# Earlier and later places for small VectorE work: the statistics of row tiles 4 and 5 and the parameters' reciprocals in a fused S4 and feed-forward kernel

## The chip, the cores and the metric

The kernel runs on one core of one Trainium2 chip. The metric is the device time of one execution in microseconds (us). A separate profiled execution gives the trace: every instruction with its engine (PE is TensorE, DVE is VectorE, ACT is ScalarE, POOL is GpSimd, SP issues DMAs), its line in the kernel, its start and its length.

## The reference

With x of 2048 rows and 576 columns, the kernel returns the sum of three terms: x, a state-space convolution of its normalised rows, and a feed-forward layer of the same rows.

```python
xn = layernorm(x)                                  # rows of 576, no scale, no shift
# S4: 128 complex states for each of the 576 channels
dt = exp(log_dt);  K[d, l] = Re(sum_n C[d, n] * dt*B[d, n] * exp(dt*A[d, n] * l))
y  = irfft(rfft(xn, 2L) * rfft(K, 2L))[:L] + xn * Dskip
# feed-forward with 4608 hidden units
f  = silu(xn @ w1) @ w2
return x + y + f
```

All inputs and outputs are float32.

## The kernel before

**The feed-forward part** sets the pace. The 2048 rows are 16 tiles of 128 rows (j = 0 to 15), in two halves of eight; a block is four tiles (512 rows). For each half, nine chunks of the hidden units are walked, each with FT = 4 groups of 128. Step `up` (lines 321 to 337) multiplies one group of w1 with a block into the PSUM tile `ph`; step `down` (338 to 356) multiplies the results with w2 into `po`, twice 288 columns for each row tile, twelve matmuls each, and VectorE adds `po` into the tile `acc` (L356).

Every product is done in three parts, since the matmul type keeps fewer bits than float32: an operand is split into a high part, rounded by ScalarE, and a low part, which VectorE obtains as a difference. So a group of w2 is loaded into `w2r` (L302, on SP's queue, two buffers), ScalarE writes `w2h` (L311), VectorE writes `w2l` (L313), and the result of `up` goes through silu `gf` (L334), `gh` (L335) and `gl` (L337). A `w2r` buffer is free for the next load when its `w2h` and `w2l` are done. The first chunk's four groups of w2 are the ones that the change calls the second weights.

**Rows.** Each pair of tiles is loaded from `x` into `acc`. `norm` (L185 to 206) takes the statistics (bn_stats L192, four for a pair; bn_aggr L193), adds epsilon (L196), has GpSimd raise to the power of -1/2 (L197) and normalises (`xn`, VectorE L201 or ScalarE L206). TensorE transposes `xn` (L124, L131), and the copies are split again (`xh` L125, `xl` L126, `x4` L133 and L134). `phase0` does that for the tiles of the first half: 0 and 1, 2 and 3, 4 and 5, 6 and 7. `late(j)` does the same for the tiles 8 to 15 (tiles `xj`, `tr`), which are written to memory for later.

**Side work.** `side` produces all other work as a generator, which `weave` runs along the feed-forward steps: each `yield` gives the share of the 288 steps at which the next part is to be emitted. `natural` computes, on tiles of 96 partitions with 6 x 128 elements (parameter layout), the magnitude, phase and decay of the S4 parameters: products and absolute values, the smaller over the larger one (three reciprocals of 96x256 each, L522; multiplied L523; cut at one L524; its square plus one L526, L527), then decays from tanh (ScalarE L531 reciprocal square root, L532 square, VectorE L535 to L537, stored by SP), then the arctangent (ScalarE L544) and the reciprocal square root (L546) of the ratio. Each `yield` in it ends a stage; the list at the end of the block below (line 906) says at which step each stage (`nt`) and each part of the late tiles (`tiles`) is emitted. `gate_of(0)`, `gate_of(1)` and `gate_of(2)` are the steps 5, 13 and 21 of 288. After it come the generator of the kernel K (`kgen`, from share 0.13) with the transform of the rows (`spread`), the product of spectra (`spectral`) and the inverse transform.

**What sets the order.** A scheduler with a timeline of its own arranges each engine's instructions when the program is built; the order on an engine is then fixed. `behind(pin)` demands that the instructions in it be issued after the instruction that is kept in `pins` under a name: `pins["xt3"]` is the last `xl`-like difference of tile 3 (L134), `pins["w2l"]` the last low part of w2 emitted so far, `pins["gl"]` and `pins["gh"]` the last results of `up`. Work inside `tc.high_priority()` (L334 to L337, L356) goes ahead of other work that is ready. ScalarE needs another table for silu than for the arctangent, and the program has an instruction (ACT_TABLE_LOAD) wherever the table changes.

Of the kernel before, what the change touches and what calls it, by code (L numbers as in the profile page):

```python
# [15 lines left out]
ALU = mybir.AluOpType  # L16
# [10 lines left out]
HD = D // 2  # L27
# [16 lines left out]
def kernel(  # L44
# [21 lines left out]
    nc = tc.nc  # L66
    FT = 4
    NCH = NFT // FT
# [43 lines left out]
    acc = {}  # L112
# [26 lines left out]
    pins = {}  # L139

    def behind(ins):
        return tc.issue_after(ins) if ins is not None else nullcontext()
# [24 lines left out]
    def load_x(j, pool, tag, engines):  # L167

        t = pool.tile([P, 2, D], F32, tag=tag, name=f"{tag}{j}")
        for i in range(2 if j == 0 else 1):  # L170
            for ps, v, eng in quarters(xv, engines):
                if j:
                    eng.dma_start(t[ps], v[:, j:j + 2])
                else:
                    eng.dma_start(t[ps, i], v[:, i])
        pairs[j] = t
        return t[:, 0, :], t[:, 1, :]
# [78 lines left out]
    def ffn():  # L256
# [82 lines left out]
        def down(blk, jj):  # L339
            half, c, b = blk  # L340
            j = 8 * half + 4 * b + jj
            js = slice(jj * P, (jj + 1) * P)
            if half == 1 and c == NCH - 1:
                if jj % 2 == 0:
                    add_conv(j, (acc[j], acc[j + 1]))
            for h in range(2):
                hs = slice(h * HD, (h + 1) * HD)
                po = ps2.tile([P, 512], F32, tag="ps2", name="po")
                n = 0
                for t in range(FT):  # L350
                    for g, w in ((0, 0), (0, 1), (1, 0)):
                        pins["pe"] = nc.tensor.matmul(po[:, :HD], G[blk, t][g][:, js], W2[half, c, t][w][:, hs],  # L352
                                                      start=n == 0, stop=n == 3 * FT - 1).ins
                        n += 1
                with tc.high_priority():
                    nc.vector.tensor_add(acc[j][:, hs], po[:, :HD], acc[j][:, hs])  # L356
            if half == 0 and c == NCH - 1:
                rows = slice(j * P, (j + 1) * P)
                nc.sync.dma_start(dr0[rows, :], acc[j])
                if j % 2:  # L360
                    acc[7 + j], acc[8 + j] = load_x(7 + j, accp, "acc", (nc.sync,))
# [103 lines left out]
    def natural(nat, par):  # L465

        fT, phiT = kf["f"], kf["phi"]
        NT, NP = 6, 96
        v = nc.vector
# [19 lines left out]
        br, bi = load(b_re, "br"), load(b_im, "bi")  # L489
# [18 lines left out]
        pr, pi, t0, t1 = tl("pr"), tl("pi"), tl("t0"), tl("t1")  # L508
# [9 lines left out]
        v.tensor_tensor(br, cr, ci, op=ALU.max)  # L518
        v.tensor_tensor(bi, cr, ci, op=ALU.min)
        v.tensor_scalar(t0, br, 1e-37, None, op0=ALU.max)  # L520
        for i in range(0, NT, 2):
            v.reciprocal(t0[:, i:i + 2], t0[:, i:i + 2])  # L522
        v.tensor_mul(t0, t0, bi)  # L523
        v.tensor_scalar(t0, t0, 1.0, None, op0=ALU.min)  # L524

        v.tensor_mul(t1, t0, t0)  # L526
        v.tensor_scalar(t1, t1, 1.0, None, op0=ALU.add)  # L527
        yield

        with behind(pins["gh"]):  # L530
# [2 lines left out]
        for i in range(0, 4 * D, D):  # L533
# [4 lines left out]
            v.scalar_tensor_tensor(r[:, c], e, 2.0, r[:, c], op0=ALU.add, op1=ALU.mult)  # L538
            v.scalar_tensor_tensor(ex[:, c], ex[:, c], 1.0, r[:, c], op0=ALU.add, op1=ALU.mult)
        nc.sync.dma_start(dexp, ex[:, :3 * D].rearrange("n (d k) -> n d k", k=3))  # L540
        yield

        with behind(pins["gh"]):
# [289 lines left out]
    def add_conv(j, dsts):  # L833

        py = [pool.tile([P, 512], F32, tag=t, name="py") for pool, t in ((pss, "pss"),) * 3 + ((ps2, "ps2"),)]
        first = pins["pe"]
        for n in range(16):
            i, q1, q2, h = 1 - n // 8, n // 4 % 2, n // 2 % 2, 1 - n % 2
            o = 64 * q1 + 32 * q2
            rows = slice(64 * h, 64 * h + 64)  # L840
            with tc.high_priority() if n else nullcontext(), behind(first):
                mm = nc.tensor.matmul(py[2 * i + h][o:o + 32, :HD], s4[rows], yss[j + i][rows, 2 * q2 + q1],  # L842
                                      start=True, stop=True, tile_position=(64 * h, o), skip_group_check=True)
            if n == 0:
                first = mm.ins
        for i in range(2):
            del yss[j + i]
            for h in range(2):
                hs = slice(h * HD, (h + 1) * HD)
                nc.vector.tensor_add(dsts[i][:, hs], py[2 * i + h][:, :HD], dsts[i][:, hs])  # L850
        for _ in range(2):
            conv_load()

    def gate_of(i):

        return (FT + i * 2 * FT + 1) / (2 * NCH * 2 * 2 * FT)

    def side():
        nonlocal s4, kl, yp, pa, tail_at
        marks = (0.13, 0.597, 0.823)  # L860
        tail_at = (0.91, 0.934, 0.967, 0.0072)
        with tc.tile_pool(name="kf", bufs=1) as kfp:
            for n in ("f", "phi"):
                kf[n] = kfp.tile([P, D], F32, name=n + "T")
            with tc.tile_pool(name="par", bufs=1) as par:
                with tc.tile_pool(name="pa", bufs=4) as pa:

                    zero = pa.tile([P, 512], BF16, name="zero", bufs=1)
                    nc.vector.memset(zero, 0.0)
                    pz = ps1.tile([P, 512], F32, tag="ps1", name="pz")  # L870

                    def idle(n):
                        for _ in range(n):
                            nc.tensor.matmul(pz, zero[:, :P], zero, start=True, stop=True)

                    idle(12)
                    p01, p23 = phase0(pa, (0, 1), idle), phase0(pa, (2, 3))
                    next(p01)
                    yield 0
                    next(p23)  # L880
                    yield 0
                    next(p01)
                    yield 0
                    next(p23)
                    yield 0
                    for js in ((4, 5), (6, 7)):
                        with behind(pins["xt3" if js[0] == 4 else "w2l"]):
                            for _ in phase0(pa, js):
                                pass
                    kf["dt"] = steps()  # L890
                    for n, ap in (("are", a_re), ("aim", a_im)):
                        kf[n] = par.tile([96, 6, NS], F32, tag=n, name=n)
                        nc.sync.dma_start(kf[n], ap.rearrange("(p t) n -> p t n", t=6))
                    yield 0
                with tc.tile_pool(name="nat", bufs=1) as nat, tc.tile_pool(name="pb", bufs=1) as pb:
                    nt = natural(nat, par)
                    def late(j):

                        xs = load_x(j, pb, "xj", (nc.sync,))
                        yield  # L900
                        with behind(pins["xn" if j == 8 else "gl"]):
                            normed(pb, (j, j + 1), xs)
                        yield

                    tiles = chain.from_iterable(late(j) for j in range(8, NJ, 2))
                    for at, todo in ((0.0, nt), (0.0, tiles), (0.004, tiles), (0.005, tiles), (gate_of(0), nt), (0.026, tiles), (0.028, tiles), (0.036, tiles), (0.038, tiles), (gate_of(1), nt), (0.06, tiles), (gate_of(2), nt), (0.09, nt)):
                        yield at
                        with behind(pins["gl"] if at else pins["xt7"] if todo is nt else None):
                            next(todo, None)
            with behind(pins["sd"]):  # L910
                nc.gpsimd.dma_start(f1, cf1)
            nc.sync.dma_start(vt, cv)
            with tc.tile_pool(name="up", bufs=1) as up:
                sp = spread(up)
                for n, at in enumerate(kgen()):
                    if n > 1:
                        next(sp, None)
                    yield marks[0] + at * (marks[1] - marks[0])
                for _ in sp:
                    pass  # L920
        s4p = ctx.enter_context(tc.tile_pool(name="s4p", bufs=1))
        s4 = s4p.tile([P, 32], F32, name="s4")
        nc.gpsimd.dma_start(s4, cs4)

        with tc.tile_pool(name="kl", bufs=2) as kl:
            for at in spectral():
                yield marks[1] + (at - 1) * (marks[2] - marks[1])
        yp = ctx.enter_context(tc.tile_pool(name="yp", bufs=3))
        yield from tail()

    sd = side()
    fg = ffn()
    for g in (sd, fg, sd, fg, sd, fg, sd, fg, sd):
# [84 lines left out]
```

## Time and profile before

| | us |
|---|---|
| median of three runs | 1111.88 (1111.85 to 1111.98) |
| the profiled execution | 1111.65 |
| its span, first to last instruction | 1109.9 |
| TensorE busy in the span | 1101.6 (99%) |
| VectorE busy | 916.1 (83%) |
| ScalarE busy | 707.3 (64%) |
| GpSimd busy | 71.0 (6%) |

The span is 1.75 us shorter than the profiled execution's own time, which is 0.23 us below the median of the runs. Times in the trace count from the start of the span. A row of a timeline gives start, length (of several merged instructions, from the first start to the last end), engine, line, operation, output and inputs, partitions x elements, count, and, in brackets, the idle time of the engine ahead of it with what ended it. Matmuls overlap: the time that one takes from the path is the distance from its start to that of the next.

### The profile page before, as it was taken

The page shows a single profiled execution, that of the slowest core. Times are in us where ns is not written, and L with a number is a line of the kernel's source. Part 1 is how long each engine was busy: PE and PEld are TensorE (multiplying, and loading weights), DVE is VectorE, ACT ScalarE, POOL GpSimd, SP SyncE. Part 2 cuts the span into 40 slices and gives each one's busy share as a digit, 9 for nine tenths or more (in the row PEclk, how much of TensorE's full clock was granted, in tenths as well). Part 3 has the DMA queues.
Part 4 walks back from the last instruction along what each step waited for, and adds up shares of the span by engine and source line. Part 5 has one row for each costly group of instructions (what it writes and reads, how often), then busy time and mean ns, then how long its engine had stood idle before and what let it go on. Part 6 is the DMA issues. An engine that isn't in the chain of part 4 may idle for free.

```text
span 1109.9 us, 22912 instructions
## 1 busy us (share of the span) xinstructions
PE 1101.6 (99%) x9167; PEld 997.5 (90%) x9167; DVE 916.1 (83%) x1542; ACT 707.3 (64%) x1223; POOL 71.0 (6%) x127
## 2 busy tenths in 40 slices
PE   8999999999999999999999999999999999999998
PEld 6988999899889899899989989999999999999887
DVE  7799899999999999999999837787778778784433
ACT  4574466676677676677866536877777778774210
POOL 1100000000000000011000000000000000000111
PEclk9999999999999999999999999999999999999999
DMA  8745522425242525255734163554544445434973
GB/s 255 205 123 154 146 61 61 120 72 126 77 109 82 130 62 130 77 154 163 209 127 105 44 177 105 168 159 126 160 145 150 139 147 170 130 107 130 257 205 87
DMA packets 175851, 148.56 MB, mean 134 GB/s; under 512 B 111088, under 2 KB 142720, under 8 KB 175616
## 3 DMA queue, kind: packets, MB, share of 16 engines
q1 hardware_dynamic: 165408, 112.69, 37.8%
q0 software_dynamic: 9504, 33.49, 9.5%
q8 instruction: 72, 1.18, 0.5%
q10 hardware_dynamic: 832, 0.92, 0.3%
q14 instruction: 35, 0.29, 0.1%
HBM read 102.53 MB, written 44.61 MB: 133 GB/s over the span
## 4 chain that ended last, share of the span: by engine, by line
PE 97%; DMA 2%; SPq 0%; DVE 0%; ACT 0%; issue 0%; ACTq 0%
PE po L352 42%; PE ph L326 35%; PE kp L691 3%; PE ph L327 3%; PE ph L328 3%; PE pu L821 2%; PE pb L821 2%; PE pk L821 2%; PE z L706 2%; PE pu L160 1%; PE py L842 1%; PE pu L161 1%; DMA acc<-in_A_u_dram 1%; DMA w2r<-in_B_w_dram 1%; DMA w1r<-in_B_w_dram 0%; PE ptk L485 0%
## 5 line engine op out<-in xcount | busy, mean ns | idle before, releaser
L352 PE MATMUL po<-w2l,gh 128*128 128x288 f32 x1152 | 338.6, 296 | 1.2 <-DVE w2l L313 1.2
L352 PE MATMUL po<-w2h,gl 128*128 128x288 f32 x1152 | 336.6, 295 | 0.0
L352 PE MATMUL po<-w2h,gh 128*128 128x288 f32 x1152 | 336.4, 296 | 0.0
L352 PEld LDWEIGHTS po<-w2h,gh 128*128 128x128 f32 x1152 | 215.3, 188 | 7.6 <-issue 2.8
L352 PEld LDWEIGHTS po<-w2l,gh 128*128 128x128 f32 x1152 | 216.0, 188 | 6.5 <-DVE w2l L313 1.4
L352 PEld LDWEIGHTS po<-w2h,gl 128*128 128x128 f32 x1152 | 215.6, 188 | 0.9
L334 ACT ACTIVATE gf<-ph 128x512 f32<-128x512 f32 (+1 forms) x148 | 86.3, 584 | 145.3 <-PE ph L328 133.0
L326 PE MATMUL ph<-xh,w1h 128*128 128x512 f32 (+1 forms) x592 | 161.6, 387 | 0.3 <-ACT xh L125 0.3
L326 PE MATMUL ph<-xl,w1h 128*128 128x512 f32 (+1 forms) x592 | 161.5, 386 | 0.0
L326 PE MATMUL ph<-xh,w1l 128*128 128x512 f32 (+1 forms) x592 | 161.2, 385 | 0.0
L356 DVE TENSOR_TENSOR acc<-po,acc 128x288 f32<-128x288 f32 x288 | 126.9, 454 | 36.9 <-PE po L352 35.6
L337 DVE TENSOR_TENSOR gl<-gf,gh 128x512 fp32r<-128x512 f32 (+1 forms) x148 | 99.4, 675 | 64.5 <-ACT gh L335 63.7
L326 PEld LDWEIGHTS ph<-xh,w1l 128*128 128x128 f32 x592 | 108.1, 188 | 19.9
L326 PEld LDWEIGHTS ph<-xl,w1h 128*128 128x128 f32 x592 | 108.0, 188 | 20.0 <-DVE xl L126 0.2
L326 PEld LDWEIGHTS ph<-xh,w1h 128*128 128x128 f32 x592 | 104.6, 188 | 17.1 <-ACT xh L125 0.8
L335 ACT CAST gh<-gf 128x512 fp32r<-128x512 f32 (+1 forms) x148 | 89.6, 609 | 9.5 <-PE po L352 6.6
L648 ACT ACTIVATE c<-th,magic 128x1040 f32<-128x1040 f32 x36 | 42.1, 1169 | 37.7 <-DVE C L671 27.7
L650 ACT ACTIVATE c<-th 128x1040 f32<-128x1040 f32 x36 | 38.7, 1075 | 34.1 <-DVE th L649 34.1
L311 ACT CAST w2h<-w2r 128x576 fp32r<-128x576 f32 x72 | 47.0, 671 | 16.7 <-PE po L352 14.9
L292 DVE TENSOR_TENSOR w1l<-w1r,w1h 128x640 fp32r<-128x640 f32 x72 | 57.2, 823 | 0.2
L327 PE MATMUL ph<-x,w1h 128*128 128x512 f32 (+1 forms) x148 | 57.1, 386 | 0.0
L328 PE MATMUL ph<-x,w1l 128*128 128x512 f32 (+1 forms) x148 | 56.9, 385 | 0.0
(182 smaller groups left out, 1829.3 us busy)
## 6 DMA issues: line engine op xcount, KB each, us to landing
w2r<-in_B_w_dram SPq DMA_DIRECT2D x72, 288.0 KB, 3.7
w1r<-in_B_w_dram SPq DMA_DIRECT2D x35, 512.0 KB, 3.7
d1u<-u POOLq DMA_DIRECT2D x32, 288.0 KB, 2.5
d1k<-stage SPq DMA_DIRECT2D x18, 512.0 KB, 7.0
ur<-d1u SPq DMA_DIRECT2D x32, 288.0 KB, 3.4
kr<-d1k SPq DMA_DIRECT2D x32, 288.0 KB, 2.8
d<-yo POOLq DMA_DIRECT2D x32, 288.0 KB, 3.6
ys<-d SPq DMA_DIRECT2D x32, 288.0 KB, 10.7
```

Source lines behind the costliest of these rows:

```text
L292: pins["w1l"] = nc.vector.tensor_sub(l1, src, h1).ins
L311: pins["w2h"] = nc.scalar.copy(h2, r2).ins
L326: nc.tensor.matmul(ph, w[:, kt, :], v[:, kt, a:e], start=n + kt == 0, stop=False)
L327: nc.tensor.matmul(ph, h1[:, 4, :], x4[:, a:e], start=False, stop=False)
L328: pins["pe"] = nc.tensor.matmul(ph, l1[:, 4, :], x4[:, a:e], start=False, stop=True).ins
L334: nc.scalar.activation(gf, ph, AF.Silu)
L335: pins["gh"] = nc.scalar.copy(gh, gf).ins
L337: pins["gl"] = nc.vector.tensor_sub(gl, gf, gh).ins
L352: pins["pe"] = nc.tensor.matmul(po[:, :HD], G[blk, t][g][:, js], W2[half, c, t][w][:, hs], start=n == 0, stop=n == 3 * FT - 1).ins
L356: nc.vector.tensor_add(acc[j][:, hs], po[:, :HD], acc[j][:, hs])
L648: nc.scalar.activation(c65, th, AF.Identity, bias=magic)
L821: nc.tensor.matmul(dst, st, mv[:, hs], start=n == 0, stop=n == 3 * len(terms) - 1)
```

## The change

Two pieces of VectorE work get other places. The statistics, normalisation and transposes of tiles 4 and 5 were to be issued behind the last difference of tile 3; now they are issued behind the low parts of the first four groups of w2, as those of tiles 6 and 7 already were. In `natural`, the three reciprocals and the four operations behind them leave the end of the second stage and become a stage of their own behind the decays and their store. That stage has a new entry in the list, three steps after `gate_of(1)` (step 16 of 288), and is issued behind the newest sum of an output into `acc` (L356), which is now kept in `pins["acc"]`. The arithmetic is the same.

```diff
@@ down
                 with tc.high_priority():
-                    nc.vector.tensor_add(acc[j][:, hs], po[:, :HD], acc[j][:, hs])
+                    pins["acc"] = nc.vector.tensor_add(acc[j][:, hs], po[:, :HD], acc[j][:, hs]).ins
@@ natural
         v.tensor_scalar(t0, br, 1e-37, None, op0=ALU.max)
-        for i in range(0, NT, 2):
-            v.reciprocal(t0[:, i:i + 2], t0[:, i:i + 2])
-        v.tensor_mul(t0, t0, bi)
-        v.tensor_scalar(t0, t0, 1.0, None, op0=ALU.min)
-
-        v.tensor_mul(t1, t0, t0)
-        v.tensor_scalar(t1, t1, 1.0, None, op0=ALU.add)
         yield
...
         nc.sync.dma_start(dexp, ex[:, :3 * D].rearrange("n (d k) -> n d k", k=3))
+        yield
+        for i in range(0, NT, 2):
+            v.reciprocal(t0[:, i:i + 2], t0[:, i:i + 2])
+        v.tensor_mul(t0, t0, bi)
+        v.tensor_scalar(t0, t0, 1.0, None, op0=ALU.min)
+
+        v.tensor_mul(t1, t0, t0)
+        v.tensor_scalar(t1, t1, 1.0, None, op0=ALU.add)
         yield
@@ side
                     for js in ((4, 5), (6, 7)):
-                        with behind(pins["xt3" if js[0] == 4 else "w2l"]):
+                        with behind(pins["w2l"]):
@@ side, the list: one entry more behind (gate_of(1), nt)
+                    (gate_of(1) + 3 / (4 * NCH * 2 * FT), nt)
-                        with behind(pins["gl"] if at else pins["xt7"] if todo is nt else None):
+                        with behind(pins["acc" if todo is nt and at == gate_of(1) + 3 / (4 * NCH * 2 * FT) else "gl"] if at else pins["xt7"] if todo is nt else None):
                             next(todo, None)
```

More of the change, by code (lines that the diff above doesn't have):

```diff
@@ L905, in side @@
                     tiles = chain.from_iterable(late(j) for j in range(8, NJ, 2))
-                    for at, todo in ((0.0, nt), (0.0, tiles), (0.004, tiles), (0.005, tiles), (gate_of(0), nt), (0.026, tiles), (0.028, tiles), (0.036, tiles), (0.038, tiles), (gate_of(1), nt), (0.06, tiles), (gate_of(2), nt), (0.09, nt)):
+                    for at, todo in ((0.0, nt), (0.0, tiles), (0.004, tiles), (0.005, tiles), (gate_of(0), nt), (0.026, tiles), (0.028, tiles), (0.036, tiles), (0.038, tiles), (gate_of(1), nt), (gate_of(1) + 3 / (4 * NCH * 2 * FT), nt), (0.06, tiles), (gate_of(2), nt), (0.09, nt)):
                         yield at
-                        with behind(pins["gl"] if at else pins["xt7"] if todo is nt else None):
+                        with behind(pins["acc" if todo is nt and at == gate_of(1) + 3 / (4 * NCH * 2 * FT) else "gl"] if at else pins["xt7"] if todo is nt else None):
                             next(todo, None)
```

## The prediction

> **What bounds the kernel now.** I read the page first: busy times, the granted clock, the chain that ended last, the DMA issues.
>
> ```profile
> PE 1101.6 (99%) x9167; PEld 997.5 (90%) x9167; DVE 916.1 (83%) x1542; ACT 707.3 (64%) x1223; POOL 71.0 (6%) x127
> ...
> PEclk9999999999999999999999999999999999999999
> ...
> PE 97%; DMA 2%; SPq 0%; DVE 0%; ACT 0%; issue 0%; ACTq 0%
> ...
> w2r<-in_B_w_dram SPq DMA_DIRECT2D x72, 288.0 KB, 3.7
> ```
>
> TensorE bounds it: 99% of the span busy, 97% of the last chain. A change of VectorE's order is worth only what TensorE waits for today, less what it makes TensorE wait for tomorrow. So next TensorE's waits over the whole run (waiter, releaser; us in total, times, longest), and TensorE's busy time in five stretches.
>
> ```profile
> PE pz L874 <- DVE zero L869: 1.3, 1, 1.3
> PE pt L124 <- DVE xn L201: 1.2, 1, 1.2
> PE po L352 <- DVE w2l L313: 1.2, 1, 1.2
> PE ph L326 <- ACT xh L125: 0.3, 1, 0.3
> ```
>
> ```profile
> 0.00:25.00 25.00, 20.88 (x132) 1.00 0.86 251
> 25.00:140.00 115.00, 115.00 (x707) 1.00 0.60 161
> 140.00:660.00 520.00, 520.00 (x5348) 1.00 0.40 107
> 660.00:1000.00 340.00, 340.00 (x2150) 1.00 0.48 145
> 1000.00:1110.00 110.00, 105.75 (x838) 1.00 0.67 171
> ```
>
> All four waits lie in the first 25 us; from 25 to 1000 us TensorE has no gap. The change touches one of the four, the third. Last the timeline around it, TensorE, then VectorE, then ScalarE's casts.
>
> ```profile
> 23.16 0.28 PE L328 MATMUL ph<-x,w1l 128*128 128x256 f32 x1
> 23.28 0.30 PE L352 MATMUL po<-w2h,gh 128*128 128x288 f32 x1
> 24.76 0.40 PE L352 MATMUL po<-w2l,gh 128*128 128x288 f32 x1 [1.18 <-DVE w2l L313]
> 25.00 0.29 PE L352 MATMUL po<-w2h,gl 128*128 128x288 f32 x1
> 25.13 0.30 PE L352 MATMUL po<-w2h,gh 128*128 128x288 f32 x1
> ```
>
> ```profile
> 20.35 0.42 DVE L134 TENSOR_TENSOR x<-pt,x 64x256 fp32r<-64x256 f32 x1
> 22.51 1.54 DVE L192 BATCH_NORM_STATS2 st<-acc 128x6 f32<-128x288 f32 x4 [1.74 <-DMA acc<-in_A_u_dram]
> 23.96 2.08 DVE L313 TENSOR_TENSOR w2l<-w2r,w2h 128x576 fp32r<-128x576 f32 x3
> 26.08 0.71 DVE L313 TENSOR_TENSOR w2l<-w2r,w2h 128x576 fp32r<-128x576 f32 x1
> 26.70 1.18 DVE L192 BATCH_NORM_STATS2 st<-acc 128x6 f32<-128x288 f32 x3
> 28.22 0.75 DVE L337 TENSOR_TENSOR gl<-gf,gh 128x256 fp32r<-128x256 f32 x2
> ```
>
> ```profile
> 19.55 2.40 ACT L311 CAST w2h<-w2r 128x576 fp32r<-128x576 f32 x4
> ```
>
> VectorE was free at 20.77 (20.35 + 0.42), idled 1.74 us for the rows of tile 4, did their statistics, and only then wrote the first w2 low part. TensorE wanted that at 23.41 (23.28 plus the pitch of 0.13 between 25.00 and 25.13) and started at 24.76.
>
> **The change part by part.** *Statistics of tiles 4 and 5.* Nothing is removed; 4 bn_stats, 2 bn_aggr and what follows go behind the four `w2l`. The casts they need end one after the other between 19.55 and 21.95, so some 0.6 us each: the first is there at about 20.2, and VectorE can start at 20.8. One `w2l` is worth 0.7 us (2.08 / 3), so the first is done at about 21.5, 1.9 us ahead of 23.41, and the last at 23.6. The wait goes. Its worth is the lost pitch: 24.76 - 23.28 - 0.13 = 1.35 us. (The matmul after the stop also began 0.24 instead of 0.13 later; that could add 0.11, which I leave in the range.)
>
> What is late next: tile 4's statistics run from 23.6 to 25.2, tile 6's and 7's after them until about 26.8, and then the `gl` that stood at 28.22. If the rows of tiles 6 and 7 came only when VectorE used them (26.70, without a wait), the `gl` would stay where it was, at 28.2 to 29.0. TensorE now does 22 output matmuls, not 9, between the first weights' products and the next group, and by their 0.13 us reaches these `gl` at about 29.1. Covered at either end, by 0.1 us in the bad one; cover gone, it costs at most 1.2 us, the size of the waits seen. The loads on SP's queue stand in the same sequence; GpSimd's two powers keep theirs. Cost: nothing.
>
> *The reciprocals.* Rows of VectorE, ScalarE, SP's queue and TensorE where the old place was and the new one is:
>
> ```profile
> 67.67 4.96 DVE L522 RECIPROCAL t<-t 96x256 f32<-96x256 f32 x3
> ...
> 78.07 0.94 DVE L523 TENSOR_TENSOR t<-t,bi 96x768 f32<-96x768 f32 x1
> ...
> 84.26 0.74 DVE L313 TENSOR_TENSOR w2l<-w2r,w2h 128x576 fp32r<-128x576 f32 x1
> ```
>
> ```profile
> 86.69 1.28 ACT L544 ACT_TABLE_LOAD   x1
> 87.99 0.85 ACT L544 ACTIVATE t<-t 96x768 f32<-96x768 f32 x1
> 88.74 0.66 ACT L311 CAST w2h<-w2r 128x576 fp32r<-128x576 f32 x1
> ...
> 93.08 1.28 ACT L334 ACT_TABLE_LOAD   x1
> 94.37 0.60 ACT L334 ACTIVATE gf<-ph 128x512 f32<-128x512 f32 x1
> ```
>
> ```profile
> 85.03 2.27 SPq L302 DMA_DIRECT2D w2r<-in_B_w_dram  x2
> ```
>
> ```profile
> 91.39 0.29 PE L352 MATMUL po<-w2h,gh 128*128 128x288 f32 x1
> ...
> 96.37 1.09 PE L326 MATMUL ph<-xh,w1h 128*128 128x512 f32 x4
> ```
>
> The work is equal: 4.96 us of reciprocals, 0.94 of a product, and three more of at most about that. VectorE has 17% of the span to spare, so its sum costs nothing; what counts is who queues behind it. In the new program order the work of decays (L535 to L537) goes ahead, and the three reciprocals start, by the lengths of what stands before them, at about 75 and end at 80. Behind them in VectorE's queue stand four bn_stats of tile 12, an output sum and then the `w2l` that frees a `w2r` buffer: about 3.2 us, so 83.2. From there the chain is load (3.7 us median by the page; this one, issued at 85.03, was cast at 88.74, so at most 3.7), cast 0.66: `w2h` at about 87.5. TensorE used these weights at 91.39; in the new order it reaches them 1.35 us earlier and another 1.9 us earlier, since six of the L326 matmuls that stood ahead now follow: 88.2. Margin 0.7 us with the long load; before it was 91.39 - 88.74 - 0.66 = 2.0.
>
> The second chain is ScalarE's queue. Eleven us of VectorE work stand between the last reciprocal and the cut to one (L524) that feeds the arctangent, so that is ready at about 91.2, where before it was not waited for at 87.99. The new order puts one silu between the arctangent and L546, so one table load more (1.28). That silu runs at 91.2 + 0.85 + 1.28, ends at 94.0, and TensorE wants its PSUM buffer free at 96.37 - 1.35 = 95.0: margin 1.0. L546 then loads its own table and the next silu once more; that silu keeps a margin of 1.4 us. With both margins positive I take nothing for it; the bound above is a wait like the three known ones, 1.2 to 1.3 us each, and below nothing, since no wait of TensorE stands there to be removed.
>
> The row says how dear a switch is: the load starts at 86.69, takes 1.28, and the arctangent starts at 87.99, 0.02 us after. The Trainium skill, page "ScalarE: Activation LUTs", section "What ACT_TABLE_LOAD costs", puts a switch at about 2.66 us, 1.28 for the load and 1.38 for a drain. By that rule the silu would be 1.38 later than I reckon and the next one 2.76, beyond both margins, and the sum would be about 1112.2, near rival C below. The trace has the 1.28 and no drain behind it, so the row decides.
>
> *The rest.* The matmuls are the same in kind and number. In the generator of K, from 140 to 660 us, the scheduler has arranged much anew, and TensorE's cover there is VectorE's:
>
> ```profile
> 189.31 0.46 DVE L356 TENSOR_TENSOR acc<-po,acc 128x288 f32<-128x288 f32 x1 [2.21 <-PE po L352]
> ...
> 389.53 1.18 DVE L356 TENSOR_TENSOR acc<-po,acc 128x288 f32<-128x288 f32 x3
> ```
>
> ```profile
> 390.04 0.40 PE L352 MATMUL po<-w2h,gh 128*128 128x288 f32 x1
> ```
>
> ```profile
> 190.00:390.00 200.00, 196.81 (x293) 1.00 0.39 100
> ```
>
> (the last row is VectorE's busy time.) For 200 us VectorE hardly rests, and at 390.04 TensorE starts within 0.1 us of the sum that frees its buffer. If VectorE didn't start earlier too, the gain would be lost there. It does: at 189.31 it waited 2.21 us for TensorE, more than 1.35, so the stretch moves along. Adding the mean lengths of the operations in both orders, VectorE's queue against TensorE's from the last such wait to the tightest sum, I find the new order about 1.2 us looser there. I cost it at nothing, with one VectorE operation of 1.2 us as the bound above.
>
> **Sum.** Span 1109.9 - 1.35 = 1108.55; with the 1.75 outside the span 1110.3, against 1111.65 for the profiled execution. The median of the runs stands 0.23 above that: 1111.88 - 1.35 = 1110.5. 0.2% of it is 2.2 us, about what a measurement of this kernel can tell from no change, so this is "no change" in that sense. Own range: 1110.3 to 1111.2 (the 0.11 more; half the gain lost).
>
> **The rivals.**
> A, *the gain is eaten*. Somewhere between 60 and 400 us one new wait of 1.2 to 2.4 us (one or two of the size seen) takes its place. For it: the margins of 0.7 and 1.0, the 0.1 at 390, an order arranged anew. Against it: no such wait in 975 us now. Time: 1111.88 - 1.35 + 1.2 = 1111.7, up to 1112.9.
> B, *slower*. The reciprocals stand 5 us in VectorE's queue ahead of the `w2l` that frees the `w2r` buffer, and of the arctangent's input, behind which ScalarE's silu is queued. Place: TensorE at 88 and at 95 us. It begins to cost when the arctangent's input is over 1.0 us later than 91.2, has eaten the gain at 2.35, and is slower by 0.2% at 1.0 + 1.35 + 2.2 = 4.55, so with an input at 95.8: that takes a whole set of reciprocals more than I counted in the queue, or the same late load again in later chunks. Time: 1114.1 to 1117.
> C, *the switch of tables is dearer than its row*: a drain as long as the load delays the silu by 1.28, 0.3 beyond its margin, and the one behind two switches by 2.56, 1.2 beyond its 1.4. Time: 1110.5 + 0.3 + 1.2 = 1112.0.
> D, *faster by over 2.2 us*: the two other waits at the start (1.2 and 0.3) go as well. They lie ahead of 23 us, where nothing is moved; only a shift of the loads could do it. Time: 1109.
> That the change doesn't do what it says is excluded: in the new order the four `w2l` stand ahead of the statistics.
>
> **How the numbers follow.** Forecast 0.61, A 0.17, B 0.16, C 0.02, D 0.04. The forecast, A and C lie within 0.2%: 0.80; slower 0.16; faster 0.04. Range 1110.0 (the forecast and its 0.11, with some scatter) to 1114.0 (where B begins); B and D, 2 in 10, are left out.
>
> **What would show it.** Right: the wait of `po` for `w2l` is gone from TensorE's waits, three remain, VectorE's rows have `w2l` x4 near 20.8 and the statistics near 23.6, and the stretch from 25 to 1000 us stays without a gap; reciprocals at 75 to 80, seven table loads in the run where there were six, and a span of 1108.5. Wrong: a TensorE row with idle time behind `w2h` or `ph` between 80 and 105 us, ended by a DMA or by ScalarE's `gf` (B, C), or one ended by `acc` or `w2l` between 140 and 400 us (A).

## The result: slower, by 8.4 us

The changed kernel takes 1120.24 us (median of six runs, 1117.89 to 1123.67) against 1111.87 us of the kernel before (six runs, 1110.72 to 1112.14): a ratio of 1.0079, with a 95% interval of 1.006 to 1.0098. The forecast was 1110.5 us, and the range ended at 1114.0. The profiled execution took 1118.97 us, near the low end of its runs, so the account of its trace below covers 7.3 of the 8.4 us.

The page of the changed kernel, the lines of the span, of busy time and of the chain that ended last:

```profile
span 1117.2 us, 22908 instructions
...
PE 1105.2 (99%) x9167; PEld 997.9 (89%) x9167; DVE 916.4 (82%) x1542; ACT 708.5 (63%) x1224; POOL 73.9 (7%) x127
...
PE 68%; DVE 15%; issue 6%; ACT 4%; DMA 4%; SPq 1%; POOL 1%; DVEq 0%; ACTq 0%; POOLq 0%
```

The engines are nearly as busy as before (TensorE 1105.2 us against 1101.6); the chain is what has changed. It ran over TensorE for 97% of the span, and now for 68%: for the rest it runs over the engines that feed TensorE. TensorE's waits, and its busy time in the first and the third of the five stretches:

```profile
PE po L352 <- DVE w2l L313: 2.2, 3, 0.8
PE po L352 <- ACT w2h L311: 1.7, 2, 1.0
PE pu L160 <- ACT stage L715: 1.6, 2, 0.8
PE pz L875 <- DVE zero L870: 1.3, 1, 1.3
PE py L843 <- DMA ys<-d: 0.5, 1, 0.5
PE po L352 <- DVE gl L337: 0.3, 1, 0.3
```

```profile
0.00:25.00 25.00, 23.55 (x147) 1.00 0.90 259
...
140.00:660.00 520.00, 514.39 (x5294) 1.00 0.41 104
```

The first 25 us hold 2.7 us more work than before (23.55 against 20.88), and the stretch from 140 to 660 us, which had no gap, has 5.6 us of gaps. TensorE's rows with 0.2 us or more of idle time ahead of them, behind 25 us and up to 660:

```profile
111.35 0.40 PE L352 MATMUL po<-w2h,gl 128*128 128x288 f32 x1 [0.27 <-DVE gl L337]
...
257.44 0.40 PE L352 MATMUL po<-w2l,gh 128*128 128x288 f32 x1 [0.81 <-DVE w2l L313]
...
383.00 0.40 PE L352 MATMUL po<-w2l,gh 128*128 128x288 f32 x1 [0.57 <-DVE w2l L313]
...
446.15 0.40 PE L352 MATMUL po<-w2l,gh 128*128 128x288 f32 x1 [0.77 <-DVE w2l L313]
...
506.36 0.40 PE L352 MATMUL po<-w2h,gh 128*128 128x288 f32 x1 [0.75 <-ACT w2h L311]
...
510.67 0.41 PE L160 MATMUL pu<-sp,s 128*128 128x288 f32 x1 [0.74 <-ACT stage L715]
...
568.57 0.53 PE L352 MATMUL po<-w2h,gh 128*128 128x288 f32 x2 [0.97 <-ACT w2h L311]
...
572.44 0.40 PE L160 MATMUL pu<-sp,s 128*128 128x288 f32 x1 [0.81 <-ACT stage L715]
```

Short delays are not listed as waits, so I also compare two traces at equal work of TensorE: each matmul counts with the median distance between starts of its form in the kernel before, these are added up along the program, and at equal sums the two start times are subtracted. Negative is ahead of the kernel before; the columns are the places by the times of the kernel before. All runs below are in the table, with one trace each.

| run | 21 us | 25 us | 107 us | 117 us | 209 us | 582 us | end |
|---|---|---|---|---|---|---|---|
| the changed kernel | -0.64 | -2.08 | -2.04 | -1.24 | -1.08 | +6.92 | +7.32 |
| e1_stats | -0.22 | -1.66 | +4.18 | +7.84 | +8.70 | +11.68 | +12.54 |
| e2_recip | -0.26 | -1.26 | +3.97 | +3.98 | +3.99 | +4.71 | +8.37 |
| e4_stats_order | -0.35 | -1.80 | -0.05 | -0.05 | -0.05 | +0.64 | +0.64 |
| e5_change_order | -0.22 | -1.66 | -1.65 | -1.41 | +3.08 | +4.26 | +4.26 |
| e6_order190 | +0.20 | -1.24 | -1.19 | -0.87 | -0.71 | -0.44 | -0.44 |
| e7_w2l_first | -0.11 | -1.55 | -1.53 | -1.38 | -1.22 | +2.25 | +3.42 |
| e8_both | -0.60 | -2.04 | -2.03 | -0.21 | +0.21 | +2.41 | +2.41 |
| e9_stats12 | -0.40 | -1.84 | -1.43 | +0.35 | +0.44 | +7.12 | +8.43 |
| e10_stats14 | +0.11 | -1.33 | -1.28 | -1.32 | -1.40 | +5.08 | +5.93 |
| e11_both14 | -0.03 | -1.47 | -1.46 | -1.49 | -1.47 | -1.62 | -1.62 |

The account of the changed kernel: 0.64 us ahead at 21 us, where nothing was changed (the other runs stand between -0.60 and +0.20 there, so that is one execution against another); 1.44 gained at 24 us; 0.8 lost at 111 us; 0.2 in small steps up to 209 us; 8.0 lost between 209 and 582 us, of which the seven waits listed there are 5.4; 0.4 behind. Together +7.3, the difference of the spans (1117.2 - 1109.9).

### The profile page after: what moved, and what is told of

It reads as the page before. It is cut to its first block, busy times and chain, and to the rows that moved or that the text cites. A ratio compares the mean times of both kernels' runs of the same rounds, so it can differ in the third digit from the quotient of the medians.

```text
span 1117.2 us, 22908 instructions
## 1 busy us (share of the span) xinstructions
PE 1105.2 (99%) x9167; PEld 997.9 (89%) x9167; DVE 916.4 (82%) x1542; ACT 708.5 (63%) x1224; POOL 73.9 (7%) x127
## 3 DMA queue, kind: packets, MB, share of 16 engines
q8 instruction: 72, 1.18, 0.5%
## 4 chain that ended last, share of the span: by engine, by line
PE 68%; DVE 15%; issue 6%; ACT 4%; DMA 4%; SPq 1%; POOL 1%; DVEq 0%; ACTq 0%; POOLq 0%
PE po L352 29%; PE ph L326 24%; PE pu L822 2%; PE pk L822 2%; PE ph L327 2%; PE ph L328 2%; PE pb L822 2%; PE kp L692 2%; DVE C L660 2%; DVE acc L356 2%; DVE gl L337 1%; DVE th L650 1%; DVE w2l L313 1%; DVE C L656 1%; PE py L843 1%
## 5 line engine op out<-in xcount | busy, mean ns | idle before, releaser
L326 PE MATMUL ph<-xl,w1h 128*128 128x512 f32 (+1 forms) x592 | 162.0, 386 | 0.0
L326 PE MATMUL ph<-xh,w1h 128*128 128x512 f32 (+1 forms) x592 | 160.4, 387 | 0.0
L326 PE MATMUL ph<-xh,w1l 128*128 128x512 f32 (+1 forms) x592 | 160.0, 385 | 0.0
L356 DVE TENSOR_TENSOR acc<-po,acc 128x288 f32<-128x288 f32 x288 | 127.5, 453 | 36.1 <-PE po L352 34.1
L326 PEld LDWEIGHTS ph<-xh,w1l 128*128 128x128 f32 x592 | 108.2, 188 | 20.6
L326 PEld LDWEIGHTS ph<-xl,w1h 128*128 128x128 f32 x592 | 107.7, 188 | 20.0 <-DVE xl L126 0.2
L326 PEld LDWEIGHTS ph<-xh,w1h 128*128 128x128 f32 x592 | 105.2, 188 | 17.7 <-issue 0.5
L313 DVE TENSOR_TENSOR w2l<-w2r,w2h 128x576 fp32r<-128x576 f32 x72 | 53.3, 753 | 8.4 <-ACT w2h L311 8.2
```

The source lines that it names most:

```text
L313: pins["w2l"] = nc.vector.tensor_sub(l2, r2, h2).ins
L326: nc.tensor.matmul(ph, w[:, kt, :], v[:, kt, a:e], start=n + kt == 0, stop=False)
L356: pins["acc"] = nc.vector.tensor_add(acc[j][:, hs], po[:, :HD], acc[j][:, hs]).ins
```

## The experiments

My theory after the result: neither of the two moves costs much where it stands. The scheduler arranges every engine's queue anew for such an edit, and the new queues feed TensorE later in places that have nothing to do with it. In the changed kernel 1631 of 7743 matmuls and 397 of 1542 VectorE instructions have changed places (those outside the longest sequence that both orders share). The rivals: the moved reciprocals themselves hold back w2 and ScalarE, or the moved statistics do.

To hold an order, the kernels with "order" in their name, and all from e6 on, end with a list of instructions for each engine, and each instruction gets an order-only dependency on the one ahead of it, of the kind that `behind` makes:

```diff
+    for names in ORDER.values():          # one list per engine
+        for prev, ins in pairwise(names):
+            tc.add_manual_dep(by[ins], prev, NoSync)
```

A list by itself gives no time back: e9_stats12 below has a list of the changed kernel's own order, but for four statistics, and takes 1120.29 us, as the changed kernel does.

**One edit each, and one edit with the old order.** e1_stats and e2_recip have half of the diff each. e4_stats_order is e1_stats with the order of the kernel before from 45 us on; e5_change_order is the whole change with it from 140 us on.

```diff
 e1_stats
-                        with behind(pins["xt3" if js[0] == 4 else "w2l"]):
+                        with behind(pins["w2l"]):
 e2_recip: the other lines of the diff, without this one
```

> Only the statistics of tiles 4 and 5 are moved; the reciprocals stay. Theory 1 (the loss is the order that the scheduler made anew for all engines, whatever edit sets it off): 1.4 us are gained at 24 us, and since 1418 of the 7743 matmuls stand elsewhere in the order too, new waits of 0.5 to 1 us appear between 140 and 640 us: 1112 to 1121 us, slower than before. Theory 2 (the moved reciprocals themselves are what delays w2 loads and ScalarE): no new waits, 1110.5 us.

> Only the reciprocals are moved; the statistics stay, so the 1.35 us at 24 us are not gained. Theory 1: new waits between 140 and 640 us in other places than in the changed kernel, 1113 to 1121 us. Theory 2: the waits of the changed kernel at the same places, 1120 us (its loss of 8 to 9 us behind 100 us without the gain).

> Only the statistics are moved, and from 45 us on every engine gets the order of the kernel before by order-only dependencies (17 of 7743 matmuls stand elsewhere, all in the first 45 us). Theory 1: the gain at 24 us stays whole, 1110.4 us, waits of TensorE at the start alone. Theory 2 says the same. If the later statistics or the load they wait for cost something of their own, 1111 us or more.

> The whole change, with the order of the kernel before from 140 us on (the reciprocals and what is around them keep their new places; 147 of 7743 matmuls stand elsewhere, all ahead of 140 us). Theory 1: what was lost behind 140 us is back; 1.4 gained at 24 us, 0.8 lost at 111 us by the late row load: 1111.2 us. Theory 2: the late w2 loads come again, 1117 us or more.

Measured against 1111.74 us of the kernel before: e1_stats 1123.97 (ratio 1.0109, 1.0095 to 1.0122), e2_recip 1118.54 (1.0057, 1.0045 to 1.0068), e4_stats_order 1112.16 (1.0002, 0.9994 to 1.0011), e5_change_order 1115.74 (1.0034, 1.0021 to 1.0047).

e1_stats, which leaves the reciprocals where they were, is the slowest of all (3 us above what was expected; e2_recip is in its range). So a loss doesn't need the moved reciprocals. Each half loses in places of its own: by the table e1_stats loses 9.5 us between 25 and 117 us and 3 more at 450, e2_recip 5.2 between 25 and 107 us and 3.7 near the end, where TensorE waits 2.3 us at 1040 us for the load of `ys`. VectorE's rows and TensorE's longest waits in e1_stats, then ScalarE's row and TensorE's longest wait in e2_recip:

```profile
66.15 3.32 DVE L522 RECIPROCAL t<-t 96x256 f32<-96x256 f32 x2
...
71.59 1.12 DVE L356 TENSOR_TENSOR acc<-po,acc 128x288 f32<-128x288 f32 x3
```

```profile
72.04 0.40 PE L352 MATMUL po<-w2h,gh 128*128 128x288 f32 x1 [2.88 <-DVE acc L356]
...
452.34 0.53 PE L352 MATMUL po<-w2h,gh 128*128 128x288 f32 x2 [2.45 <-ACT w2h L311]
```

```profile
94.36 0.85 ACT L545 ACTIVATE t<-t 96x768 f32<-96x768 f32 x1
```

```profile
101.82 1.31 PE L326 MATMUL ph<-xh,w1h 128*128 128x512 f32 x4 [2.81 <-ACT gf L334]
```

Even so, the reciprocals are at work in the first loss of either. In e1_stats, where they keep their stage, the new order puts three sums behind them that stood ahead of them (71.59 us, against 66.58 in the kernel before), and TensorE waits for these sums. In e2_recip the arctangent behind them starts 6.4 us later than in the kernel before (94.36 against 87.99), and the `gf` that TensorE waits for is queued behind it: that is the second chain of the prediction, in rival B. The changed kernel, with both moves, loses under 0.1 us between 25 and 107 us. What a place of the reciprocals costs thus depends on the order around them, and the halves do not add up (12.2 and 6.8 us alone, 8.4 together).

e4_stats_order missed what I expected: the gain at 24 us was there (1.45, from -0.35 to -1.80) and gone at 67 us. TensorE's row, then VectorE's of the same run, then VectorE's of the kernel before:

```profile
67.21 0.41 PE L352 MATMUL po<-w2h,gh 128*128 128x288 f32 x1 [1.12 <-DVE acc L356]
```

```profile
66.72 1.17 DVE L356 TENSOR_TENSOR acc<-po,acc 128x288 f32<-128x288 f32 x3
```

```profile
66.58 1.18 DVE L356 TENSOR_TENSOR acc<-po,acc 128x288 f32<-128x288 f32 x3
```

TensorE came 1.8 us earlier, VectorE 0.14 later: ahead of 67 us VectorE works through the parameters and does not follow TensorE. The first edit alone, in the old order, runs into the three sums that stand there. In the changed kernel VectorE comes to these sums at 64.20 us, 2.4 us earlier, and TensorE keeps its lead past 100 us:

```profile
64.20 1.17 DVE L356 TENSOR_TENSOR acc<-po,acc 128x288 f32<-128x288 f32 x3
```

e5_change_order also came out above what I expected, by 4.5 us. Its trace loses 4.4 us at one place, behind the start of the order that was taken over (ScalarE's rows first, then TensorE's):

```profile
142.33 0.67 ACT L155 CAST sp<-xr 64x576 fp32r<-64x576 f32 x1 [0.85 <-DMA xr<-dxn]
...
146.07 1.07 ACT L651 ACTIVATE c<-th 128x1040 f32<-128x1040 f32 x1 [3.06 <-DVE th L650]
```

```profile
149.83 1.76 PE L326 MATMUL ph<-xh,w1h 128*128 128x512 f32 x4 [2.08 <-ACT gf L334]
```

The parameters are finished later with the reciprocals' new place: they are stored at 128.72 instead of 127.40 us, and the loads behind that on SP's queue go out 1.8 us later. In the old order ScalarE waits for these loads, 2.27 us at 139 us, and then `sp` starts at 142.33 us, 3.3 us later than in the kernel before. VectorE waits for `sp` ahead of an angle `th`, ScalarE for `th`, and the `gf` that TensorE needs stands behind that. So the move has a cost of its own where the two orders meet. Behind that, from 209 to 582 us, it loses 1.2 us, where the changed kernel loses 8.0.

**The seam moved, and the changed kernel with one thing put right.** e6_order190 takes the old order from 190 us on, where VectorE waited for TensorE anyway. e7_w2l_first holds the changed kernel's own order and moves 24 `w2l` and 9 loads:

```diff
 VectorE's list, for each w2l between 220 and 640 us that starts over 0.3 us behind its w2h
-    ..., w2h's end, 1 to 10 other instructions, w2l, ...
+    ..., w2h's end, w2l, the other instructions, ...
 SP's list: the load that waits for it, likewise
```

> The whole change; up to 190 us every engine keeps the order of the changed kernel, from 190 us on it gets that of the kernel before. At 200 us the changed kernel stood 1.1 us ahead of the kernel before. Theory 1 (the order behind it is what loses 7.9 us): TensorE stays ahead, but for up to 1 us at 440 us, where the runs with this order have waited for a w2 load; 1111.0 to 1111.7 us. Rival (the changed kernel is late there for a reason that the order does not hold, such as later loads or a lower clock): 1117 us or more.

> The changed kernel with its own order on every engine, but 24 low parts of w2 between 220 and 640 us moved up in VectorE's queue to where their high part is ready (by 0.4 to 6 us), and 9 loads of w2 moved up on SP's queue accordingly; TensorE's and ScalarE's orders are untouched. Theory 1 in its exact form (VectorE's queue holds the w2l back, they hold back the loads into the two w2r buffers, and TensorE waits for what is loaded): the waits for w2l and w2h at 257, 382, 446, 506 and 568 us go, and the waits for ScalarE's stage copies right behind two of them; 1113 to 1115 us. Rival (the loads are slow by contention, or VectorE is simply full there): the waits stay or move to the sums and low parts that are now later; 1118 us or more.

Measured against 1111.75 us: e6_order190 1112.06 (1.0, 0.9991 to 1.0009), e7_w2l_first 1115.11 (1.0033, 1.002 to 1.0045), 0.1 above its range. All of TensorE's waits in e6_order190:

```profile
PE pz L875 <- DVE zero L870: 1.3, 1, 1.3
PE ph L326 <- ACT xh L125: 0.6, 1, 0.6
PE pt L124 <- DVE xn L201: 0.5, 1, 0.5
```

None of them lies behind 15 us; the wait at 440 us that I allowed for is not there, but the median is 0.4 us above my range. From 209 us to the end it loses 0.3 us instead of 8.4: nearly the whole loss of that stretch is the order. e7_w2l_first shows what in the order. The rows of the changed kernel around its wait at 568 us, ScalarE, VectorE, SP's queue, ScalarE again:

```profile
556.22 1.24 ACT L311 CAST w2h<-w2r 128x576 fp32r<-128x576 f32 x2
```

```profile
562.30 1.42 DVE L313 TENSOR_TENSOR w2l<-w2r,w2h 128x576 fp32r<-128x576 f32 x2
```

```profile
563.07 1.00 SPq L302 DMA_DIRECT2D w2r<-in_B_w_dram  x2
```

```profile
567.84 0.67 ACT L311 CAST w2h<-w2r 128x576 fp32r<-128x576 f32 x1 [1.87 <-DMA w2r<-in_B_w_dram]
```

The high parts were ready at 557.5; VectorE's queue came to the low parts at 562.3, since sums, angles and two `gl` stood ahead; the load that needs their buffer went out at 563.1 and landed at 567.8; the cast ended at 568.5 and TensorE started at 568.57, 0.97 us late. ScalarE's queue was held up meanwhile, and the wait for its stage copy at 572.44 follows. With the `w2l` moved up, the waits for `w2h` and for the stage copies are gone, and of those for `w2l` one is left, at 383 us, which I had expected to go too; two short ones for sums are new:

```profile
PE po L352 <- DVE w2l L313: 0.6, 1, 0.6
PE po L352 <- DVE acc L356: 0.5, 2, 0.3
```

From 209 to 582 us the loss is 3.5 us instead of 8.0 (e9_stats12 and e10_stats14, which keep the changed kernel's order there, lose 6.7 and 6.5). By the medians e7_w2l_first is 3.4 us over the kernel before instead of 8.4. About half of the loss was this chain, then; the sums that now stand behind the `w2l` take part of the gain, and what makes up the remaining 3.5 us I have not separated. The share of the last chain is no measure of the loss: it is 98% TensorE in e6_order190, but 54% in e7_w2l_first, less than in the slower changed kernel.

**The 0.8 us at 111 us.** VectorE's rows of the changed kernel, at the start, at the reciprocals and ahead of that wait:

```profile
20.16 2.77 DVE L313 TENSOR_TENSOR w2l<-w2r,w2h 128x576 fp32r<-128x576 f32 x4
22.85 2.97 DVE L192 BATCH_NORM_STATS2 st<-acc 128x6 f32<-128x288 f32 x8
25.74 0.74 DVE L337 TENSOR_TENSOR gl<-gf,gh 128x256 fp32r<-128x256 f32 x2
...
74.32 4.96 DVE L536 RECIPROCAL t<-t 96x256 f32<-96x256 f32 x3
...
106.09 0.82 DVE L192 BATCH_NORM_STATS2 st<-xj 128x6 f32<-128x288 f32 x2 [3.60 <-DMA xj<-in_A_u_dram]
...
110.62 0.68 DVE L337 TENSOR_TENSOR gl<-gf,gh 128x512 fp32r<-128x512 f32 x1
```

VectorE stood 3.6 us at the statistics of tiles 14 and 15 ("tile 14" below, as "tile 12" stands for 12 and 13), whose rows had not landed, and the `gl` that TensorE wanted was behind them. The loads of these rows went out from 100.76 us, in the kernel before from 95.64. I first took the statistics of tile 12, behind the reciprocals, for the reason of the late rows:

```diff
 e9_stats12, and e8_both likewise on top of e6_order190 (with three w2l near 375 us moved up)
-    reciprocal, reciprocal, reciprocal, acc, 4 bn_stats of tile 12
+    reciprocal, 4 bn_stats of tile 12, reciprocal, reciprocal, acc
```

> The changed kernel in its own order, but for the four bn_stats of tile 12, which go behind the first of the three reciprocals. If the late rows of tile 14 are what TensorE lost 0.8 us to at 111 us, that loss is gone or under 0.2 us and VectorE's 3.6 us of waiting for the rows at 106 us shrink to under 1; the waits behind 220 us stay, 1119 us. If not, the loss at 111 us is 0.8 as before, 1120 us.

> The kernel of the run with the old order from 190 us on, and in it the four bn_stats of tile 12 moved from behind the three reciprocals to behind the first of them, and three low parts of w2 near 375 us moved up. If the 0.4 us lost at 111 us there come from the rows of tile 14, which are loaded late because tile 12's statistics stand behind the reciprocals, they are not lost now: TensorE stays 1.2 to 1.4 us ahead of the kernel before to the end, 1110.5 us against its 1111.75. If that loss has another cause, 1111.5 us or more.

Measured: e9_stats12 1120.29 (ratio 1.0081, 1.0061 to 1.0102), e8_both 1114.42 (1.0021, 1.0011 to 1.0031), against 1111.62. Neither brought the gain that I expected. In e9_stats12 VectorE waits 1.35 us for tile 12's rows between the reciprocals, and about as long as before, 3.49 us, for tile 14's:

```profile
77.63 1.54 DVE L192 BATCH_NORM_STATS2 st<-xj 128x6 f32<-128x288 f32 x4 [1.35 <-DMA xj<-in_A_u_dram]
```

Both lose 1.8 us between 107 and 117 us. e8_both loses 1.2 more at 382 us, where its three `w2l` were moved and TensorE now waits 0.5 us for `gh` and 0.2 for `gl`; e11_both14 below, without that move, loses nothing there, so the move seems to have cost this.

The next two leave the rows late and take VectorE's queue out of their way; e11_both14 has it on top of e6_order190:

```diff
 e10_stats14, e11_both14
-    4 bn_stats, 2 bn_aggr, epsilon of tile 14 (among sums and products), gl, gl
+    sums and products, gl, gl, 4 bn_stats, 2 bn_aggr, epsilon of tile 14
```

> The changed kernel in its own order, but the four bn_stats of tile 14, their two bn_aggr and the addition of epsilon, which VectorE met at 102.4 us and waited 3.6 us for (the rows had not landed), go behind the second of the two gl that stood at 110.6 and 111.3 us. The statistics of tile 12 were not what made the rows late, as the run before showed; if the blocked VectorE queue is still what TensorE lost 0.8 us to at 111 us, that loss is now under 0.1 us. If it is 0.8 again, the loss has another cause. The rest stays as in the changed kernel, 1119 us.

> The same seven instructions moved in the kernel with the old order from 190 us on. If both readings hold (the old order loses next to nothing behind 190 us; the blocked queue is the loss at 111 us), TensorE stays 1.2 to 1.4 us ahead of the kernel before, so far as the row loads of the first 15 us come at the same time: 1110.5 us against 1111.7. If not, 1111.7 or more.

Measured against 1111.55 us: e10_stats14 1118.0 (1.005, 1.0033 to 1.0066), e11_both14 1110.77 (0.999, 0.9981 to 0.9998). VectorE in e10_stats14, and all of TensorE's waits in e11_both14:

```profile
106.78 1.28 DVE L337 TENSOR_TENSOR gl<-gf,gh 128x512 fp32r<-128x512 f32 x2
107.98 1.53 DVE L192 BATCH_NORM_STATS2 st<-xj 128x6 f32<-128x288 f32 x4
```

```profile
PE pz L875 <- DVE zero L870: 1.3, 1, 1.3
PE pt L124 <- DVE xn L201: 0.4, 1, 0.4
PE ph L326 <- ACT w1h L290: 0.3, 1, 0.3
```

The `gl` come 3.8 us earlier, and the loss between 107 and 117 us is gone in both runs (-1.28 to -1.32, -1.46 to -1.49). The runs that keep the changed kernel's order there wait 2.9 to 3.6 us for the rows and lose 0.15 to 0.8 us, the most where the wait is longest. In its trace e11_both14 keeps the 1.44 us of the first edit to the end. By the medians, with the whole change and the seven moved instructions in it, it is 0.8 us faster than the kernel before, and the interval of the ratio excludes 1.

## Why the prediction was wrong, by its steps

*The statistics*: right. TensorE's wait for `w2l` is gone, the four `w2l` run from 20.16 us and the statistics from 22.85 to 25.82. The gain was put at 1.35 with 0.11 more possible; all runs that have the edit gain 1.44 or 1.45 between the first two columns. The `gl`, feared at 28.2, came at 25.74. One thing the sum took for fixed is not: e2_recip, without this edit, waited 0.18 us instead of 1.18 at that place (at 23.50 us), since the rows of tile 4 kept VectorE waiting 0.73 us and not 1.74 in that execution.

*The reciprocals*: right in the changed kernel that nothing is lost there, in part by luck. They ran from 74.32 to 79.28 (forecast 75 to 80), the `w2h` behind them ended at 85.9 (87.5), and neither of the two chains that I bounded made TensorE wait. VectorE's row, then ScalarE's:

```profile
89.35 0.94 DVE L540 TENSOR_TENSOR t<-t 96x768 f32<-96x768 f32 x1
```

```profile
90.33 0.85 ACT L545 ACTIVATE t<-t 96x768 f32<-96x768 f32 x1 [1.96 <-DVE t L540]
91.19 1.28 ACT L334 ACT_TABLE_LOAD   x1
92.49 0.60 ACT L334 ACTIVATE gf<-ph 128x512 f32<-128x512 f32 x1
```

The arctangent started at 90.3 (forecast 91.2), after a wait of 1.96 us, and the silu behind it ended at 93.1 (94.0). That these times are close is luck: the cut to one, which the forecast took for the input, ended at 87.41, and the wait was for the square (L540), which reads the tile that the arctangent overwrites. In the first chain six of the L326 matmuls are 1.4 us and not 1.9 (four take 0.91, from 92.41 to 93.32 us in the kernel before); nothing hung on it. And in e2_recip, in another order, the second chain did make TensorE wait. The table load takes 1.28 and the silu starts 0.02 later: rival C did not happen. The drain that the Trainium skill gives on the page "ScalarE: Activation LUTs", section "What ACT_TABLE_LOAD costs", does not show in this trace. What I left out of the queue behind the reciprocals is the row path: the statistics of tile 14 stood in VectorE's queue ahead of their rows. That cost 0.8 us at 111 us.

*The rest* is the step that failed: "I cost it at nothing, with one VectorE operation of 1.2 us as the bound above." It cost 8.0 us between 209 and 582. The count behind it, VectorE's lengths against TensorE's, ended at the sum at 389.53 us and found the new order 1.2 us looser up to there. By the comparison above the changed kernel had lost 2.2 us of the 8.0 by 390 us, and lost 5.8 behind, where nothing was counted. The count also took every instruction as ready when its queue reached it. It left out that a `w2l` frees a buffer, that a load then takes 3.7 us in the median, and that a cast follows; VectorE's sum of work may be the same and this chain still be late. The prediction had that chain, for one load, with a margin of 0.7 us; it recurs for each of the 72 groups of w2, and the new order had it late five times: at 257, 383 and 446 us TensorE waited for the `w2l` itself, at 506 and 568 us for the `w2h` behind the load. Rival A named the mechanism, waits in an order arranged anew, and bounded it at one or two waits; there were seven and many shorter delays. The two at 257 and 383 us are the sign that the prediction gave for A. Rival B's place, 88 and 95 us, was not it, though its "same late load again in later chunks" was; the measured 1120.24 us lies beyond its 1117.

## What to carry to other kernels

Where a scheduler fixes the order, a small edit is two changes: the edit, and a new draw of every queue. Price the second from what the kernel before has no room for: walk each chain from a freed buffer through its load to its use, in every repetition, and see how much of it the new order shifts. To learn what an edit itself is worth, hold the rest of the order, with the place where the two orders meet chosen with care (e5_change_order lost 4.4 us there), and compare traces at equal work of the bounding engine; and look whether the next engine follows when that one gets ahead (at 67 us it did not).

## What the runs showed that was not expected

The two halves of the change, alone, cost 12.2 and 6.8 us in a kernel where TensorE had no gap in 975 us; the first half with the order held cost nothing that can be measured (1112.16 against 1111.74). And the time from issue to landing spreads widely for loads of one size, the 288 KB of a group of w2. The line of the w2 loads (L302) between 480 and 640 us, in the changed kernel and in the kernel before:

```profile
DMA to landing us min/median/max: 2.9/4.7/8.9
```

```profile
DMA to landing us min/median/max: 2.7/3.8/8.0
```

The load that TensorE waited for at 568 us, sent out at 563.07, took 4.8 us. A load of the upper end that an order sends out late leaves that much less room; which loads land late, and why, no run here shows.
